# Moving the issue of 28 value-cache tiles from the SyncE queue to GpSimd's queue in a decode-attention kernel

## Chip, core and metric

One core of one Trainium2 chip runs the whole kernel. The metric is the device time of that core in microseconds (us), as a median of runs.

## What is computed

One token (`x`, 448 wide) attends to a key and value cache of 8 heads with 65536 positions of 256 bf16 numbers; each cache head serves two query heads. Beside it runs a small gated feed-forward layer, and a gate `g` mixes the two.

```python
q = (x @ wq)                                # 16 query heads of 256, 8 cache heads
scores = einsum("bhqd,bhkd->bhqk", q, k) * (Dh ** -0.5)
p = softmax(scores)                         # over 65536 positions
o = einsum("bhqk,bhkd->bhqd", p, v)
a = o.reshape(B, Sq, Hq * Dh) @ wo
h = relu(x @ W_gate) * (x @ W_up);  b = h @ W_down
return g * a + (1 - g) * b                  # g = sigmoid(sum(x * gate_w))
```

The two caches are 268 MB each; every byte of them is read once.

## The kernel before

**Tiles and buffers.** Each head's cache is cut into 4 K tiles and 4 V tiles of 128 partitions x 32768 bf16 (8.39 MB, one contiguous 64 KB row per partition), so there are 32 K tiles and 32 V tiles, called K0 to K31 and V0 to V31 here. SBUF holds three such buffers, `ring[0]` to `ring[2]` (L301). `place` (L406) puts K tile n in `ring[1 + n % 2]`, V tiles 0 to 27 in `ring[0]`, and the last four V tiles, for which no K tile is left, in `ring[1]` and `ring[2]`; `wo` comes into `ring[0]` at the end. The weights `wq`, `W_down`, `W_gate` and `W_up` pass through `ring[0]` before V0.

**What is done with a tile.** A K tile is transposed in place by VectorE in four pieces (L529); then TensorE multiplies it with the queries ("QK", L540, 64 matmuls into `ST`), VectorE takes the maximum (L703), and ScalarE the exponential (L705). After the fourth K tile of a head, `P_sb` is rescaled and transposed into `ptp` ("the end of the head", L715 to L760). A V tile needs a slice of `ptp` copied by ScalarE (`pcur`, L591, which also waits for the tile to land) and then 64 matmuls into `O` ("PV", L584).

**What sets the order.** Every operation has a key, a planned time, and each engine's program is sorted by it. On TensorE, K and V work alternate one to one: PV of V0, QK of K4, PV of V1, QK of K5, and so on; V tile i stands beside K tile i + 4. All transfers of tiles are issued by SyncE on one queue, also alternating: K, V, K, V. Before it issues a tile, SyncE waits for TensorE to be done with the tile that had its buffer (`free`, L564): for K tile n the QK of tile n - 2 (L680), for V tile i the PV of tile i - 1 (L772). As SyncE issues in order, a V tile whose buffer isn't free also holds up the K tile behind it.

**Semaphores.** A transfer raises the semaphore of its buffer (`d_r0`, `d_r1`, `d_r2`) by 16. The counts that the other engines wait for are worked out from the plan; TensorE's and ScalarE's inner part is a hardware loop whose wait values are held in registers.

**End.** V28 and V29 wait for the QK of K30 and K31, V30 for the PV of V28; V31 is cut in three pieces (L776) that wait for the PV of V29, and `wo` in six (L785).

The few lines that the prediction follows:

```python
680  kd = dma("sp", t, "r%d" % sl, lambda e: e.dma_start(ring[sl][:], k_src(n)), free(("k", n)))
772  dep = dma("sp", t, "r%d" % sl, lambda e: e.dma_start(ring[sl][:], v_src(n)), free(("v", n)))
567  out_.append(l_[f] if isinstance(f, str) else qk[f[1], 1] if f[0] == "k" else pv[f[1]])
```

Of the kernel before, what the change touches and what calls it, by code (L numbers as in the profile page):

```python
# [27 lines left out]
class _Plan:  # L28
# [14 lines left out]
    def dma(self, eng, key, sem, fn, deps=()):  # L43
        if sem not in self.dsem:
            self.dsem[sem] = self.es.enter_context(self.nc.semaphore("d_" + sem))
        o = _Op(eng, key, fn, deps, dma=sem)
        self.ops.append(o)
        return o
# [212 lines left out]
def bass_gated_mix__gqa_block_cached__glu_gated_reglu__decode_kernel(  # L261
# [22 lines left out]
    NTH = S // TK  # L284
    NT = H * NTH
# [11 lines left out]
    with es:  # L297
# [3 lines left out]
        ring = [sb("ring%d" % i, [128, U * DH], BF) for i in range(NRING)]  # L301
# [69 lines left out]
        op, dma = pl.op, pl.dma  # L371
# [23 lines left out]
        t = 3.0  # L395
# [10 lines left out]
        def place(kind, i):  # L406
            if kind == "k":
                return 1 + i % 2
            if kind == "v":
                return 1 + i % 2 if i >= NT - NTH else 0  # L410
            return {"vp": 2, "wo": 0}[kind]

        for kind, i, _ in order:
            if kind in ("k", "v") or (kind, i) in (("wo", 0), ("vp", 0)):
                r = place(kind, i)
# [105 lines left out]
        def v_src(i):  # L521
            h, a = divmod(i, NTH)
            return A_v_cache[0, h, :, :].rearrange("(t g p u) d -> g p t (u d)", t=NTH, g=NTH, u=U)[a]
# [40 lines left out]
        def free(key):  # L564
            out_ = []
            for f in freed[key]:
                out_.append(l_[f] if isinstance(f, str) else qk[f[1], 1] if f[0] == "k" else pv[f[1]])
            return out_
# [55 lines left out]
        for kind, i, t in sorted(issue, key=lambda q: q[0] != "wq"):  # L624
# [51 lines left out]
            elif kind == "k":  # L676
                n = i
                h, t_ = divmod(n, NTH)
                sl = slot["k", n]
# [88 lines left out]
            elif kind in ("v", "vp"):  # L768
                if kind == "v":
                    n, lo, hi = i, 0, U  # L770
                    sl = slot["v", n]
                    dep = dma("sp", t, "r%d" % sl, lambda e, sl=sl, n=n: e.dma_start(ring[sl][:], v_src(n)), free(("v", n)))  # L772
                else:
                    n, (lo, hi) = NT - 1, PIECES[i]
                    sl = slot["vp", 0]
                    dep = dma("sp", t, ("wq", "wqh", "wd")[i], lambda e, sl=sl, n=n, lo=lo, hi=hi: e.dma_start(  # L776
                        ring[sl][:, lo * 256:hi * 256], v_src(n)[:, :, lo * 256:hi * 256]), free(("vp", 0)))
                args = (n, lo, hi, sl, tL[kind, i], dep)
                if ("tev", n // NTH) in last:
                    make_pv(*args)  # L780
                else:
                    pending.append(args)
            elif kind == "wo":
                lo, hi = WO[i]
                l_["wo", i] = dma("sp", t, "wo%d" % i, lambda e, lo=lo, hi=hi: e.dma_start(  # L785
                    wo_sb[:, lo:hi, :], A_wo.rearrange("(p s) n -> p s n", s=32)[:, lo:hi, :]), free(("wo", 0)))
# [89 lines left out]
```

## Time and profile before

| what | value |
|---|---|
| device time, median of 3 runs | 1275.85 us (1275.74 to 1276.02) |
| profiled execution, first to last instruction (its span) | 1274.3 us |
| difference of the two | 1.55 us |
| bytes moved | 549.13 MB, 431 GB/s over the span |
| DMA queue of SyncE (q1), share of 16 DMA engines' span | 99.7% |
| PE, DVE, ACT, POOL busy | 29%, 49%, 6%, 0% |

The page gives the span of the profiled execution; a device time of that one execution isn't listed apart, so the median stands for it, 1.55 us above. PE is TensorE's matmuls, PEld its weight loads, DVE VectorE, ACT ScalarE, POOL GpSimd, SP SyncE; a name with a q (SPq, ACTq) is the engine's instruction queue, where DMAs are issued. "idle <-X" names what an engine's wait ended on. In rows by window, the last two numbers are the mean busy share of the 16 DMA engines and GB/s; packets are booked in the window in which they start, with their whole time and bytes, so in a very short window the share counts starts and can be far above 1.

### The profile page before, as it was taken

What the parts mean: (1) busy time and instruction counts of PE and PEld (TensorE: products, weight loads), DVE (VectorE), ACT (ScalarE), POOL (GpSimd) and SP (SyncE); (2) the same over time, 40 slices, a digit from 0 to 9 for tenths busy, and PEclk for the clock granted to TensorE, in tenths of its full rate; (3) what the DMA queues carried; (4) which work ended last, traced back from release to release, by engine and by line L of the source; (5) the groups of instructions that cost most, each with busy time, mean ns of one, the idle gap of its engine ahead of it and who ended that gap; (6) DMA issues with size and microseconds to landing.
All of it is one profiled execution on the core that took longest, in us unless ns stands there. A gap on an engine that the chain in (4) does not pass through costs nothing.

```text
span 1274.3 us, 10240 instructions
## 1 busy us (share of the span) xinstructions
PE 365.9 (29%) x4497; PEld 151.4 (12%) x4505; DVE 630.1 (49%) x309; ACT 78.0 (6%) x163; POOL 4.6 (0%) x23
## 2 busy tenths in 40 slices
PE   0534321133320332312233222323302332112525
PEld 0101110011110111101111110111100111001201
DVE  4777655553455633557433565335654355553300
ACT  0001100010000100001000010000000010000100
POOL 1000000000000000000000000000000000000000
PEclk9766665666655666656666656666566666566667
DMA  9999999999999999999999999999999999999998
GB/s 411 430 436 432 426 430 434 432 443 432 430 432 432 434 442 430 430 434 430 438 438 430 430 434 430 440 438 428 430 434 430 444 434 428 430 436 430 442 421 369
DMA packets 11389, 549.13 MB, mean 431 GB/s; under 512 B 1267, under 2 KB 1654, under 8 KB 2294
## 3 DMA queue, kind: packets, MB, share of 16 engines
q1 hardware_dynamic: 11378, 549.03, 99.7%
q8 instruction: 4, 0.07, 0.0%
q14 instruction: 3, 0.02, 0.0%
q10 hardware_dynamic: 4, 0.00, 0.0%
HBM read 549.03 MB, written 0.00 MB: 431 GB/s over the span
## 4 chain that ended last, share of the span: by engine, by line
DMA 81%; PE 16%; DVE 2%; ACT 1%; issue 1%; SPq 0%; ACTq 0%
DMA ring<-in_A_v_cache_dram 74%; PE O L584 13%; DMA ring<-in_A_wo_dram 3%; DMA ring<-in_A_wq_dram 2%; DMA ring<-in_A_k_cache_dram 2%; DVE ring L529 1%; PE ST L540 1%; ACT pcur L591 1%; PE O L501 1%; PE A_ps L551 0%; SPq L785 0%; SPq L776 0%; PE O L653 0%; DVE ring L660 0%; PE A_ps L653 0%
## 5 line engine op out<-in xcount | busy, mean ns | idle before, releaser
L529 DVE STREAM_TRANSPOSE ring<-ring 128x4096 uint32<-128x4096 uint32 x128 | 557.6, 4413 | 196.9 <-DMA ring<-in_A_k_cache_dram 196.9
L584 PE MATMUL O<-ring,pcur 128*4 128x512 bf16 x2048 | 187.3, 545 | 790.4 <-ACT pcur L591 781.9
L703 DVE TENSOR_REDUCE nmb<-ST 128x1 f32<-128x512 f32 x32 | 22.1, 692 | 345.9 <-PE ST L540 345.9
L584 PEld LDWEIGHTS O<-ring,pcur 128*4 128x4 bf16 x2048 | 59.3, 111 | 914.8 <-ACT pcur L591 794.6
L540 PE MATMUL ST<-ring,xcur 128*16 128x512 bf16 x2048 | 136.7, 420 | 44.3 <-DVE ring L529 43.7
L540 PEld LDWEIGHTS ST<-ring,xcur 128*16 128x16 bf16 x2048 | 62.4, 92 | 112.1 <-DVE ring L529 48.6
L705 ACT ACTIVATE P_sb<-ST,nmb 128x512 bf16<-128x512 f32 x32 | 44.6, 1392 | 368.3 <-DVE nmb L703 368.3
L591 ACT COPY pcur<-ptp 128x256 bf16<-128x256 bf16 x32 | 13.2, 415 | 732.6 <-DMA ring<-in_A_v_cache_dram 732.6
L607 DVE TENSOR_SCALAR o_sb<-O,rcm 128x256 bf16<-128x256 f32 x8 | 3.8, 479 | 61.1 <-PE O L584 61.1
L730 DVE TENSOR_TENSOR P_sb<-P_sb,hs 128x1024 bf16<-128x1024 bf16 x16 | 18.9, 1222 | 8.1 <-ACT hs L724 8.1
L735 PE MATMUL PT<-identb,P_sb 128*128 128x128 bf16 x128 | 14.5, 282 | 17.6 <-DVE P_sb L730 17.3
L501 PE MATMUL O<-ring,P_sb 128*128 128x512 bf16 x28 | 8.5, 477 | 17.3 <-DMA ring<-in_A_wq_dram 17.3
L735 PEld LDWEIGHTS PT<-identb,P_sb 128*128 128x128 bf16 x128 | 10.7, 127 | 19.9 <-DVE P_sb L730 19.9
L744 ACT COPY ptp<-PT 128x256 bf16<-128x256 bf16 x32 | 10.3, 375 | 23.0 <-PE PT L735 23.0
L705 ACT ACTIVATION_READ_ACCUMULATOR P_sb<-ST,nmb 128x1 f32 x32 | 8.3, 258 | 0.0
L501 PEld LDWEIGHTS O<-ring,P_sb 128*128 128x128 bf16 x28 | 3.2, 117 | 22.2 <-issue 20.5
L551 PE MATMUL A_ps<-ring,attnA 128*1 128x224 bf16 x64 | 5.3, 322 | 1.1 <-DMA ring<-in_A_wo_dram 1.0
L719 PE MATMUL M_ps<-identf,hs 128*2 128x128 f32 x8 | 2.3, 283 | 10.0 <-DVE hs L717 10.0
L756 DVE RECIPROCAL rc<-M_ps 128x2 f32<-128x2 f32 x8 | 1.4, 171 | 7.5 <-PE M_ps L755 7.5
L755 PE MATMUL M_ps<-hs,ones_f 128*128 128x2 f32 x16 | 4.5, 352 | 0.0
L722 PE MATMUL M_ps<-mx,nselT 2*128 2x1 f32 x16 | 3.2, 268 | 3.0 <-DVE mx L721 3.0
L755 PEld LDWEIGHTS M_ps<-hs,ones_f 128*128 128x128 f32 x16 | 4.0, 311 | 0.0
(93 smaller groups left out, 68.6 us busy)
## 6 DMA issues: line engine op xcount, KB each, us to landing
ring<-in_A_v_cache_dram SPq DMA_DIRECT2D x1, 4096.0 KB, 22.1
ring<-in_A_wq_dram SPq DMA_DIRECT2D x1, 3072.0 KB, 28.9
ring<-in_A_v_cache_dram SPq DMA_DIRECT2D x1, 3072.0 KB, 28.8
ring<-in_B_W_down_dram SPq DMA_DIRECT2D x1, 1568.0 KB, 53.0
ring<-in_B_W_gate_dram SPq DMA_DIRECT2D x1, 1344.0 KB, 26.3
ring<-in_B_W_up_dram SPq DMA_DIRECT2D x1, 1344.0 KB, 29.2
ring<-in_A_wo_dram SPq DMA_DIRECT2D x1, 1232.0 KB, 33.0
ring<-in_A_v_cache_dram SPq DMA_DIRECT2D x1, 1024.0 KB, 30.7
```

Source lines behind the costliest of these rows:

```text
L501: ins = e.matmul(QN_ps, xw3[:, kt, 31 - m:159 - m], rhs, start=(kt == 0 and m == 0), stop=(kt == R3 and m == J // 4 - 1))
L529: return lambda e: e.transpose(v, v)
L540: ins = e.matmul(bank[32 * w:32 * w + 16, :], xcur[:, x0:x0 + 16], ktv[sl][:, u0:u0 + 16, c, :, r_], start=(b == 0 and c == 0 and r_ == 0) ...
L551: ins = e.matmul(A_ps[32 * g:32 * g + 1, 0:D2], lhsT, rhs[:, g * D2:(g + 1) * D2], start=start, stop=stop, skip_group_check=True, tile_pos ...
L584: ins = e.matmul(OP[32 * g:32 * g + 4, :], pcur[a % 2][:, 4 * k:4 * k + 4], ring[sl][:, k * 512:(k + 1) * 512], start=False, stop=False, s ...
L591: pc[n] = op("ap", max(tp - 5, last["tev", h] - 0.5), lambda e: e.copy(pcur[a % 2][:].rearrange("p (k i) -> p k i", i=4), ptp[:].rearrange ...
L703: smax[n] = op("dv", sx, lambda e, n=n, t_=t_: e.tensor_reduce(NM[:, t_:t_ + 1], ST[n % 2][:], AX.X, ALU.max, negate=True), [qk[n, 1], las ...
L705: aexp[n] = op("ac", sx + 1, lambda e, n=n, t_=t_: e.activation(P_sb[:, t_:2048:4], ST[n % 2][:], ACTF.Exp, bias=NM[:, t_:t_ + 1], scale=1 ...
L730: rsc = op("dv", tt, lambda e, pb=pb: e.tensor_tensor(pb, pb, X[:, 12:16].unsqueeze(1).to_broadcast([128, 256, 4]), ALU.mult), [h7, aexp[n]])
L735: ins = e.transpose(PT[rd][:, s * 128:(s + 1) * 128], P_sb[:, (rd * 8 + s) * 128:(rd * 8 + s + 1) * 128], identb[:, :])
L744: ins = e.copy(dst, src)
L755: l3 = mop("pe", T + 19, lambda e: e.matmul(LS_ps, ones_f[:, :], X[:, 6:8], start=True, stop=True), [l2, c_one], tag="l3")
```

## The change

V tiles 0 to 27 are issued by GpSimd (`"gp"`) with semaphores of their own name (`d_v0` in place of `d_r0`, since all 28 lie in `ring[0]`); V28 to V30 stay with SyncE, as do the three pieces of V31. The waits before each issue (`free`) stay what they were. NT - NTH is 28.

```diff
                 if kind == "v":
                     n, lo, hi = i, 0, U
                     sl = slot["v", n]
-                    dep = dma("sp", t, "r%d" % sl, lambda e, sl=sl, n=n: e.dma_start(ring[sl][:], v_src(n)), free(("v", n)))
+                    dep = dma("gp" if n < NT - NTH else "sp", t, ("v%d" if n < NT - NTH else "r%d") % sl, lambda e, sl=sl, n=n: e.dma_start(ring[sl][:], v_src(n)), free(("v", n)))
                 else:
```

SyncE's instructions before, from the last weights on (s_pe counts QK, s_pv counts PV and other work of TensorE; the rows go on alternating K and V):

```order
L640 DMA ring<-in_B_W_up_dram 128x5376
L642 DMA ring<-in_B_W_up_dram 128x896
L680 DMA ring<-in_A_k_cache_dram 128x32768 [waits s_pe] x2
L772 DMA ring<-in_A_v_cache_dram 128x1x32768 [waits s_pv]
L680 DMA ring<-in_A_k_cache_dram 128x32768 [waits s_pe]
```

SyncE's instructions with the change, at the same place and on to the pieces of V31:

```order
L640 DMA ring<-in_B_W_up_dram 128x5376
L642 DMA ring<-in_B_W_up_dram 128x896
L680 DMA ring<-in_A_k_cache_dram 128x32768 [waits s_pe] x29
L772 DMA ring<-in_A_v_cache_dram 128x1x32768 [waits s_pe] x2
L772 DMA ring<-in_A_v_cache_dram 128x1x32768 [waits s_pv]
L776 DMA ring<-in_A_v_cache_dram 128x1x16384 [waits s_pv]
L776 DMA ring<-in_A_v_cache_dram 128x1x12288
L776 DMA ring<-in_A_v_cache_dram 128x1x4096
```

Nothing stands between the K tiles any longer: each waits for the QK that frees its buffer and for no V tile, and V28 follows right behind K31.

GpSimd's instructions with the change, from the last of its set-up on (the buffer's number shown):

```order
L457 TENSOR_TENSOR selc<-selc 128x1 [waits s_gp]
L458 TENSOR_TENSOR selc<-selc 128x1 [waits s_gp]
L459 TENSOR_TENSOR selc<-selc 128x1 [waits s_gp]
L460 TENSOR_SCALAR selc<-selc 128x2 [waits s_gp]
L461 TENSOR_SCALAR selc<-selc 128x2 [waits s_gp]
L772 DMA ring0<-in_A_v_cache_dram 128x1x32768 [waits s_pv] x28
L808 UNCONDITIONAL_BRANCH
```

The 28 V tiles now stand behind GpSimd's set-up, which had been its whole program, each with the wait for the PV before it. TensorE's and VectorE's programs are unchanged; on ScalarE one register instruction falls away, since it waits for another semaphore.

## Prediction

> **What bounds the kernel now.** I read the page's slices first, then its queues, then the share of one long stretch.
>
> ```profile
> DMA  9999999999999999999999999999999999999998
> GB/s 411 430 436 432 426 430 434 432 443 432 430 432 432 434 442 430 430 434 430 438 438 430 430 434 430 440 438 428 430 434 430 444 434 428 430 436 430 442 421 369
> ...
> q1 hardware_dynamic: 11378, 549.03, 99.7%
> ...
> q10 hardware_dynamic: 4, 0.00, 0.0%
> ```
> ```profile
> 300.00:1100.00 800.00, 214.96 (x2805) 91.58 (x2798) 397.88 (x169) 48.85 (x102) 0.00 (x0) 0.62 1.00 434
> ```
>
> The DMA engines have no gap from start to end: share 1.00 at 434 GB/s, while no other engine is busy for half of the stretch. So any microsecond in which they stand still is added to the time, and nothing else is. How they are kept full is seen in the chain of work (start, duration) and in SyncE's own instructions.
>
> ```profile
> 457.27 32.13 DMA ring<-in_A_v_cache_dram
> ...
> 489.43 0.42 ACT pcur L591
> ...
> 495.36 32.74 DMA ring<-in_A_v_cache_dram
> ...
> 528.20 0.42 ACT pcur L591
> ...
> 528.66 6.54 PE O L584 x63
> ...
> 535.21 31.59 DMA ring<-in_A_v_cache_dram
> ```
> ```profile
> 495.36 0.55 SPq L772 DMA_DIRECT2D ring<-in_A_v_cache_dram  x1
> 499.01 0.33 SPq L680 DMA_DIRECT2D ring<-in_A_k_cache_dram  x1
> 535.21 0.55 SPq L772 DMA_DIRECT2D ring<-in_A_v_cache_dram  x1
> 538.93 0.33 SPq L680 DMA_DIRECT2D ring<-in_A_k_cache_dram  x1
> ```
> ```profile
> ring<-in_A_v_cache_dram SPq DMA_DIRECT2D x31, 32.2
> ```
>
> A V tile lands, PV runs, and only then is the next V tile issued. V tiles land 38.7 us apart (from 141.10 for V0 to 1186.11 for V27, below: 1045.0 / 27 = 38.70); the transfer's median is 32.2, so **6.5 us** lie between a landing and the next V issue. The next K issue follows 3.7 us later (499.01 - 495.36, 538.93 - 535.21), since QK stands behind PV on TensorE. In these 6.5 us the DMA engines are fed by the K tile that was issued 3.7 us behind the V tile and passes behind it, whole: two tiles in 38.7 us are 19.35 us each, and the V tile's last byte is followed by 19.35 us of K. That cover is what the strict order buys.
>
> **How two queues share the engines.** One place shows it: ScalarE's queue (q10) loads the two small vectors while K0 passes on SyncE's. Issues, landings and 0.25 us windows of the start:
>
> ```profile
> 0.72 0.42 SPq L680 DMA_DIRECT2D ring<-in_A_k_cache_dram  x1
> ```
> ```profile
> 1.27 0.21 ACTq L422 DMA_DIRECT2D scr<-in_gate_w_dram  x1
> ```
> ```profile
> 10.15 0.61 DVE L464 TENSOR_TENSOR ptp<-P_sb,scr 1x448 f32<-1x448 bf16 x1 [3.93 <-DMA scr<-in_gate_w_dram]
> ...
> 22.81 17.42 DVE L529 STREAM_TRANSPOSE ring<-ring 128x4096 uint32<-128x4096 uint32 x4 [8.20 <-DMA ring<-in_A_k_cache_dram]
> ...
> 102.40 17.42 DVE L529 STREAM_TRANSPOSE ring<-ring 128x4096 uint32<-128x4096 uint32 x4 [1.22 <-DMA ring<-in_A_k_cache_dram]
> ```
> ```profile
> 1.75:2.00 0.25, 0.00 (x0) 0.00 (x0) 0.25 (x1) 0.00 (x0) 0.23 (x1) 1.00 6.44 2097
> ...
> 4.75:5.75 1.00, 0.27 (x5) 0.21 (x5) 0.55 (x4) 0.00 (x0) 0.76 (x4) 1.00 2.42 1049
> 5.75:7.25 1.50, 0.00 (x0) 0.00 (x0) 0.40 (x3) 0.00 (x0) 0.65 (x4) 1.00 0.00 0
> 7.25:7.50 0.25, 0.00 (x0) 0.00 (x0) 0.00 (x0) 0.00 (x0) 0.00 (x0) 1.00 4.24 1839
> ...
> 9.50:10.50 1.00, 0.00 (x0) 0.00 (x0) 0.35 (x1) 0.00 (x0) 0.00 (x0) 1.00 2.42 1049
> ```
>
> 2097 GB/s x 0.25 us are eight packets of 65536 bytes: a packet is one partition's 64 KB row, each of the 16 engines has 8 rows of a tile, and starts come in waves of 16 (1049 GB/s x 1 us), 2.42 us apart (19.35 / 8). `gate_w` was issued at 1.27; its 0.9 KB start only at 7.25 to 7.50 (1839 is seven rows, 1835, and 1 KB), and it counts as landed at 10.15, after a further wave. That reads as strict turns on an engine: `x`, a row of K0, the completion of `x`, a row, `gate_w`, a row, its completion; q10 has four packets. So I take **one 64 KB row per turn, and a turn of its own for the completion**.
>
> [...]
>
> **The change, worked out.** Nothing is removed: same bytes, waits and work. The issue moves from SyncE (0.55 us each) to GpSimd, whose program had 4.6 us of work in all, done by 5 us. K is no longer held behind V. From K0: issued 0.72, first rows 1.75 to 2.00 (1.0 later), landed 22.81, which is 22.1 after the issue, 19.35 for rows and **2.7** around them.
>
> K first runs ahead. While both pass in turns they have equal rates, and in V's 6.5 us K has all of it, so K gains until both K buffers are full and K n + 2 can be issued only behind QK of K n, which stands behind a PV on TensorE. Then a cycle is, from a V landing: 6.5 us to the next V issue; K's issue 3.7 later. V's first row takes 3.1 (starts 1.75, then 4.85, the second wave), so its second is under way when K arrives. Then K, V in turns: K1 V3 K2 V4 ... K6 V8 K7, and V's completion. That is 8 + 7 rows, 15 x 2.42 = 36.3, with 2.7 around them: 6.5 + 2.7 + 36.3 = **45.5 us a cycle instead of 38.7**. One K row is left as cover, and 6.8 us a cycle the DMA engines stand still. K's transposes (17.4 us) begin after the maximum, at 11, and at a head's end about 9 later, so they are done long before the next QK; PV is what K waits for.
>
> Start: V0 is issued behind the weights as before.
>
> ```profile
> 104.18 36.90 DMA ring<-in_A_v_cache_dram
> 141.10 0.04 ACTq L166
> ...
> 147.16 32.62 DMA ring<-in_A_v_cache_dram
> 179.81 0.42 ACT pcur L591
> ...
> 1186.11 0.42 ACT pcur L591
> ...
> 1224.80 0.42 ACT pcur L591
> ```
>
> K3 landed at 102.40, so two rows of K4 are gone by 106.8 when V0 gets its first turn; eight turns each with K4 and K5, 38.7, end at 145.5, and V0 lands at 145.9 (141.1 before). V1 is issued at 152.4 and gets its turn at 155.2, after four rows of K5 alone, with no gap; 16 turns later, at 194.3, it lands (179.8 before: +14.5). From V1 to V27 are 26 cycles of 45.5: V27 lands at 1377.3, before at 1186.1, +191.2. Tail: V29 waits for PV of V27 and QK of K31, 6.5 + 3.7, and takes 22.1 alone: it lands 32.3 behind V27 where 38.7 was (1224.80 - 1186.11), -6.4; the rest stays. Sum against the profiled execution: 1274.3 + 191.2 - 6.4 = 1459.1, and with the 1.55 us between its span and the median of the runs **1460.7**.
>
> **What the trace doesn't show.** GpSimd issues no DMA before, so its delay from wait to first row is open. Lower end: no issue time, -0.55 us a cycle. Upper end: the shares of 16 engines written one after another at its mean instruction (4.6 us / 23 = 0.2), +3.2.
>
> ```profile
> PE 365.9 (29%) x4497; PEld 151.4 (12%) x4505; DVE 630.1 (49%) x309; ACT 78.0 (6%) x163; POOL 4.6 (0%) x23
> ```
>
> I take SyncE's own delay, the nearest row. If V comes more than 0.6 us later (3.7 - 3.1), K's first row stands second, and all eight K rows pass within V's: 47.9 and the delay. If the completion costs no turn, it is 43.1. [...]
>
> **Rivals.**
> First, on the other side: **a whole V tile in one turn.** Then V passes in 19.35, the K tile issued behind it is left whole and covers the 6.5 + 2.7, the engines never stand still: 38.7 a cycle, 1276, no change. It decides from four K rows left at V's landing (9.2 / 2.42 = 3.8). Against it are the waves above; for it, that GpSimd's packets were never seen. [...]
> Second: **K goes faster than V**, if V's rows come in smaller packets. Then V ends alone behind all of K, with no cover: 47.9 a cycle, 26 x 2.4 = 62 more, 1523.
> Third: **two queues move more than one.** Were 434 the limit of one queue, and the best slice (444) what two reach, with the cover kept, 1045 us would shrink by 2.3%, 24 us: 1252. Against it: share 1.00, rows back to back.
>
> **How the numbers follow.** Forecast 0.70 (1398 with a free completion, 1461 - 26 x 2.4; 1549 with a delay of 1.0, 1461 + 26 x 3.4), second rival 0.17, inside that span; first rival 0.09, third 0.04. So the range is 1395 to 1550; 0.13 and some of the delay's upper end stay out. 0.2%, about what a measurement here can tell from no change, is 2.6 us. Faster 0.05 (third rival, and a little of the first), same 0.06, slower 0.89.
>
> **What would show it.** Right: DMA share near 0.85 (38.7 / 45.5), about 370 GB/s in the middle; V landings 45 us apart; K landing 2 to 4 us behind V; SyncE's K issue waiting for QK in each cycle and TensorE never waiting for transposes. Wrong: share 1.00 and 38.7 us cycles (first rival); K landing well before V with V alone at the end (second); above 434 GB/s (third); or another engine late.

## The result, and the profile after

The changed kernel takes 1473.19 us (median of 4 runs, 1467.32 to 1475.78) against 1275.93 before (1275.74 to 1276.10): **1.154 times as long, 95% interval 1.1519 to 1.156**. 1460.7 was predicted. The profiled execution has a span of 1465.2 us and is the fastest of the four (1467.32).

The page after, its slices and queues:

```profile
DMA  9999988898888988879888798888978889888798
GB/s 415 423 449 428 431 349 344 372 430 338 349 354 361 424 349 370 344 345 429 370 344 345 344 429 356 360 344 370 426 324 369 347 367 419 356 356 340 335 412 376
...
q1 hardware_dynamic: 7346, 314.15, 49.7%
q0 software_dynamic: 4032, 234.88, 38.4%
...
q10 hardware_dynamic: 4, 0.00, 0.0%
```

The first five slices are much as before; from V1's cycle on most fall to some 340 to 370 GB/s, and those near 430 are the ones into which hardly any standstill falls. GpSimd's queue appears as q0 with 4032 packets: 28 tiles x 128 rows and 28 x 16 completions, so its packets are 64 KB rows too, like SyncE's. A long stretch in the middle (share and GB/s last; before 1.00 and 434):

```profile
300.00:1300.00 1000.00, 226.83 (x2992) 96.72 (x2993) 423.95 (x184) 51.51 (x110) 11.62 (x22) 0.60 0.87 368
```

One cycle in the chain of work after: V lands, ScalarE's copy, PV, GpSimd's issue, V under way again.

```profile
566.54 39.09 DMA ring<-in_A_v_cache_dram
605.63 0.02 issue
605.65 0.04 ACTq L166
605.69 0.04 issue
605.73 0.42 ACT pcur L591
606.15 0.04 issue
606.20 6.39 PE O L584 x64
612.59 0.28 issue
612.88 39.14 DMA ring<-in_A_v_cache_dram
```

The V transfer's own time is 39.1 us where it was 32.2, and this cycle is 46.3 long (612.88 - 566.54). The mean is 45.7: V1 lands at 194.90 and V27 at 1382.71 (below), 1187.8 / 26. Where the DMA engines stand still is seen in windows of the same cycle:

```profile
604.00:605.00 1.00, 0.00 (x0) 0.00 (x0) 0.00 (x0) 0.00 (x0) 0.00 (x0) 0.50 0.61 262
605.00:606.00 1.00, 0.00 (x0) 0.00 (x0) 0.00 (x0) 0.27 (x1) 0.00 (x0) 0.50 1.82 786
606.00:608.00 2.00, 1.80 (x20) 0.66 (x24) 0.00 (x0) 0.14 (x1) 0.00 (x0) 0.50 0.00 0
608.00:612.00 4.00, 4.00 (x48) 1.29 (x40) 0.00 (x0) 0.00 (x0) 0.00 (x0) 0.53 0.00 0
612.00:614.00 2.00, 2.00 (x42) 0.89 (x37) 0.00 (x0) 0.00 (x0) 0.53 (x1) 1.00 0.00 0
614.00:614.25 0.25, 0.25 (x12) 0.12 (x8) 0.00 (x0) 0.00 (x0) 0.00 (x0) 1.00 8.38 2621
```

Sixteen rows (1.0 MB: 0.26 + 0.79) start between 604 and 606, about when V lands: K's last row on each engine. It is done by about 608, and until 614.0 no row starts, while TensorE runs PV. K's rows cover 2.4 us of the gap and no more.

The trace's DMA records, counted by queue, show the turns themselves. For the tile issued at 566.54, V starts its first row on all 16 engines at 567.8 to 568.8 and its second at 570.9 to 571.6; from 573.3 on each engine starts a row of K after each row of V, 2.42 us apart, until V's eighth. On 9 of the 16 engines K has the third turn, on 7 V has it. On those 7 the 4-byte record of V's completion stands at 602.3 to 603.0, on the 9 at 604.8 to 605.2, each behind a further row of K: the tile lands with its last engines, one row later.

Who waits for whom (DVE's and SyncE's waits):

```profile
DVE ring L529 <- DMA ring<-in_A_k_cache_dram: 26.6, 6, 7.8
```
```profile
SPq L680 <- PE ST L540: 1285.3, 30, 46.5
```

The transposes wait for K 26.6 us in all (196.9 before), and SyncE's K issues wait 1285.3 us in all for QK (191.1 before), 30 of 32, all but the first two. So K is ahead as far as its two buffers allow.

### The profile page after: what moved, and what is told of

The parts are those of the page before. It is cut to its first block, busy times and chain, and to the rows that moved or that the text cites. A ratio compares the mean times of both kernels' runs of the same rounds, so it can differ in the third digit from the quotient of the medians.

```text
span 1465.2 us, 10241 instructions
## 1 busy us (share of the span) xinstructions
PE 363.6 (25%) x4505; PEld 149.0 (10%) x4505; DVE 628.2 (43%) x309; ACT 78.0 (5%) x163; POOL 19.6 (1%) x51
## 3 DMA queue, kind: packets, MB, share of 16 engines
q0 software_dynamic: 4032, 234.88, 38.4%
## 4 chain that ended last, share of the span: by engine, by line
DMA 80%; PE 13%; issue 4%; DVE 1%; ACT 1%; SPq 0%; ACTq 0%; POOL 0%; POOLq 0%
DMA ring<-in_A_v_cache_dram 74%; PE O L584 11%; DMA ring<-in_A_wo_dram 2%; DMA ring<-in_A_wq_dram 2%; DMA ring<-in_A_k_cache_dram 2%; DVE ring L529 1%; PE ST L540 1%; ACT pcur L591 1%; PE O L501 1%; PE A_ps L551 0%; SPq L776 0%; DVE ring L660 0%; PE O L653 0%; PE A_ps L653 0%; ACTq L166 0%
## 5 line engine op out<-in xcount | busy, mean ns | idle before, releaser
L529 DVE STREAM_TRANSPOSE ring<-ring 128x4096 uint32<-128x4096 uint32 x128 | 557.3, 4411 | 28.1 <-DMA ring<-in_A_k_cache_dram 26.6
L584 PE MATMUL O<-ring,pcur 128*4 128x512 bf16 x2048 | 183.4, 536 | 979.8 <-ACT pcur L591 973.4
L772 POOL DMA_DIRECT2D ring<-in_A_v_cache_dram x28 | 15.0, 536 | 1322.2 <-PE O L584 1226.5
L571 PE MATMUL O<-zer,identb 128*128 128x512 bf16 x8 | 4.7, 587 | 0.0
```

The source lines that it names most:

```text
L529: return lambda e: e.transpose(v, v)
L584: ins = e.matmul(OP[32 * g:32 * g + 4, :], pcur[a % 2][:, 4 * k:4 * k + 4], ring[sl][:, k * 512:(k + 1) * 512], start=False, stop=False, s ...
L772: dep = dma("gp" if n < NT - NTH else "sp", t, ("v%d" if n < NT - NTH else "r%d") % sl, lambda e, sl=sl, n=n: e.dma_start(ring[sl][:], v_s ...
```

## The experiments

All times are medians of the kernel's runs. Two theories stand against each other. **Turns**: on each DMA engine the queues take turns packet by packet, so K is spent beside V and nothing covers PV. **GpSimd**: its way of issuing is slow in itself.

**One queue, but GpSimd's.**

```diff
-kd = dma("sp", t, "r%d" % sl, ...)
+kd = dma("gp" if n >= 3 else "sp", t, ("g%d" if n >= 3 else "r%d") % sl, ...)
-dep = dma("sp", t, "r%d" % sl, ...)
+dep = dma("gp", t, ("g%d" if sl else "v%d") % sl, ...)
```

> All tiles from K3 on, K and V alike up to V30, are issued by GpSimd in the old strict order; SyncE keeps the weights, the three pieces of V31 and wo. Theory of turns (the loss comes from K and V taking turns row by row, so that K is nearly spent when V lands): with one queue again, V passes whole and the K tile behind it is the cover. The 0.28 us that GpSimd takes from PV's end to the issue lie under that cover. 1276 us, at most 1285 with the pieces of V31 passing beside V30. Rival (GpSimd's own way of issuing makes transfers slower or later): all 61 tiles now bear that cost, so as slow as the change or slower, 1470 or more.

Measured: 1289.13 us, 1.0102 of before (1.0086 to 1.0119).

```profile
110.00:120.00 10.00, 0.00 (x0) 0.00 (x0) 0.00 (x0) 0.00 (x0) 0.00 (x0) 0.50 0.79 343
120.00:130.00 10.00, 5.87 (x61) 2.69 (x61) 5.20 (x5) 0.00 (x0) 0.00 (x0) 0.50 0.00 1
...
300.00:1100.00 800.00, 220.09 (x2838) 92.66 (x2838) 393.99 (x168) 49.25 (x103) 22.16 (x42) 0.62 1.00 433
```

In the middle the share is 1.00 at 433 GB/s: GpSimd's issue costs nothing there. The 13 us over before, 4 beyond the expectation, come from a place that it had missed: K3 and K4 on the new queue took turns with `W_gate` and `W_up` on SyncE's, these landed late, V0 was issued at 130.5, and some 12 us stood empty. The same turns, at another spot.

**K in half rows, V in half rows, both.** K from K4 on, V tiles 0 to 27:

```diff
-kd = dma("sp", t, "r%d" % sl, lambda e: e.dma_start(ring[sl][:], k_src(n)), ...)
+for q_ in range(2):
+    kd = dma("sp", t + 0.001 * q_, "r%d" % sl, lambda e: e.dma_start(
+        ring[sl][:, q_ * 16384:(q_ + 1) * 16384], k_src(n)[:, q_ * 16384:(q_ + 1) * 16384]), ...)
```

> The change, but each K tile from K4 on is issued as two DMAs of half rows (32 KB per partition), both on SyncE's queue; V tiles keep 64 KB rows on GpSimd's. Theory of turns, one packet per turn: V now moves two bytes for each of K's. In a cycle V's 8 rows are met by only some 7 half rows of K, so about 9 half rows (10.9 us) are left when V lands, more than the 9.5 us without V: no standstill, cycles of about 38.7 us, 1280 to 1300 us. Rival (the queues share by bytes, or GpSimd's issue itself costs the time): no change from 1473, or a little more for 28 more packets of DMA.

> The opposite: each V tile on GpSimd's queue is issued as two DMAs of half rows (32 KB per partition), K tiles keep 64 KB rows. Theory of turns: K moves two bytes for each of V's, all of K passes within V's span and nothing is left as cover; a cycle is 6.8 + 2.7 + 38.7 = 48.2 us instead of the 45.7 measured, 26 x 2.5 = 65 us more than the change: about 1535 us. Rival (sharing by bytes, or a fixed cost per V tile at GpSimd): 1473, or a few us more for the second issue of 0.53 us per tile (28 x 0.53 = 15): up to 1490.

> K tiles from K4 on and V tiles 0 to 27 are both issued as two DMAs of half rows. Theory of turns: turns are equal again, only half as long. V passes 3 half rows before K's first, then 13 of V against 13 of K and the completion's turn: two or three half rows of K are left, 2.4 to 3.6 us, as with one whole row; cycles of 45 to 46 us: 1455 to 1480 us. Rival (issuing K in two parts helps by itself, whatever V's rows are): near the 1296 us of K alone in halves.

Measured: K halves 1295.92 us (ratio 1.0146 to 1.018), V halves 1535.44 (1.2012 to 1.2052), both 1439.45 (1.1269 to 1.1307). The issues (count, KB, us to landing) of K halves, then of V halves:

```profile
ring<-in_A_k_cache_dram SPq DMA_DIRECT2D x56, 4096.0 KB, 36.8
...
ring<-in_A_v_cache_dram POOLq DMA_DIRECT2D x28, 33.0
```
```profile
ring<-in_A_v_cache_dram POOLq DMA_DIRECT2D x56, 4096.0 KB, 37.0
```

The bytes and the two queues are the same in all three; halving K's packets brings V down from 39.1 to 33.0 us and the time back to within 2% of before, halving V's adds 62 us to the change (65 expected). In these runs the rate goes by packets, not by bytes. With both halved the time is 16 us below the low end expected: in most cycles of that run V lands 37.7 us behind its first issue, 1.5 us earlier than in the change (39.2), and 26 x 1.5 = 39 covers the 34 us between 1473 and 1439. The step that the expectation had wrong is the start: by the DMA records of two cycles V passes four or five half rows before K's first, by engine, and not three. Of the 20 us that K halves keeps above before, some 10 are in the tail, where V29 waits for PV and QK and no row starts from 1210 to 1220 us.

**K held back by its own transposes.**

```diff
-kd = dma("sp", ..., free(("k", n)))
+kd = dma("sp", ..., free(("k", n)) + ([last["tr"]] if n > NTH else []))
 tr = [op("dv", tk + 4.5 * w, f_trans(sl, w), [kd]) for w in range(4)]
+last["tr"] = tr[1]
```

> The change, but SyncE holds each K tile from K5 on until VectorE has done two of the four transposes of the K tile before it, some 9 us later than now (18 at a head's end). Nothing else differs. Theory of turns: V passes some 5 rows alone, so about 4 or 5 K rows are left when V lands (9.7 to 12 us), enough to cover the 9.5 us without V: cycles near 38.7 us, except at heads' ends, where K comes late and some 3 us stand still 7 times: 1280 to 1310 us. Rival (GpSimd's issue itself costs the time, or simply that K waits too long): a later K can only add: 1473 or more, up to 1473 + 27 x 9 = 1716.

> The late K of the run before, but the hold begins with K8, when K has run ahead. Theory of turns, with the 47 us that the slices of 130 to 300 us lost there put down to the hold itself (from K5 on it kept a single K tile under way, which landed beside V): the start is now as in the change (V landings about 145, 195 and 240 us), then no standstill except at heads' ends and at the tail: 1300 to 1320 us. Rival (the excess of the late K over 1276 is spread over all cycles): 1344 as before, or the change's extra at the start on top, up to 1360.

 (here the condition is `n >= 2 * NTH`)

Measured: 1343.72 us and 1368.37 us. Both expectations missed, the second in its reason too. The late K, by stretches:

```profile
100.00:300.00 200.00, 56.67 (x603) 19.82 (x603) 93.11 (x36) 9.40 (x20) 2.88 (x5) 0.59 0.84 356
...
500.00:900.00 400.00, 129.81 (x1340) 42.02 (x1340) 196.88 (x78) 21.79 (x46) 5.30 (x10) 0.62 0.99 423
```

From 500 us on it does what was said: share 0.99 where the change has 0.87. At its start it doesn't. GpSimd's V issues there, SyncE's K issue beside the second of them, and the stretch before it:

```profile
148.00 0.54 POOL L773 DMA_DIRECT2D ring<-in_A_v_cache_dram  x1 [45.18 <-PE O L584]
195.63 0.53 POOL L773 DMA_DIRECT2D ring<-in_A_v_cache_dram  x1 [47.09 <-PE O L584]
```
```profile
194.77 0.33 SPq L680 DMA_DIRECT2D ring<-in_A_k_cache_dram  x1
```
```profile
187.00:195.00 8.00, 6.18 (x64) 2.07 (x68) 8.00 (x3) 0.42 (x1) 0.00 (x0) 0.52 0.00 0
```

K is issued 0.9 us before V: the two start together, pass in turns, land together, and both gaps fall together (no row starts from 187 to 195), in a cycle of 47.6 us (195.63 - 148.00). Since a held K follows its own landing by some 9 us and V its own by some 7, K drifts behind V from cycle to cycle; by V7 it is 10 us behind, and its rows cover the gap. The five runs of the second hold lie from 1364.5 to 1452.7, and the trace is of the longest: there K drifts until it meets the next V at 564 us and stays with it for a dozen cycles of 47.7 us. How far that holds for the shorter runs isn't shown. So the hold was a wait of its own, and these two runs say little on the question.

**The queues swapped.**

```diff
-kd = dma("sp", t, "r%d" % sl, ...)
+kd = dma("gp" if n >= 4 else "sp", t, ("g%d" if n >= 4 else "r%d") % sl, ...)
```

(V tiles stay with SyncE, as before the change.)

> The two queues swapped: K tiles from K4 on are issued by GpSimd, all V tiles by SyncE. Theory of turns: which queue carries which makes no difference, since each gets one row per turn; only V's issue no longer bears GpSimd's 0.28 us behind PV (SyncE: 0.02), 27 x 0.26 = 7 us less than the change: about 1466 us. Rival (GpSimd's queue is served worse than SyncE's, in rate or delay): now K is the slow one, more of it is left when V lands, and the time falls well below, under 1420 us.

Measured: 1405.21 us (ratio 1.0989 to 1.1026): 68 below the change, on the rival's side. Two issues of V, which SyncE makes, in the chain:

```profile
552.91 37.02 DMA ring<-in_A_v_cache_dram
...
596.41 37.02 DMA ring<-in_A_v_cache_dram
```

V takes 37.0 us, not 39.1: 2.1 us, about one row (2.4). The swap has moved K's issue from 3.4 us behind V's (616.27 - 612.88 in the change) to 4.0 us. Either GpSimd's queue is served worse, or 4.0 us is late enough for V to pass one row more alone. The next three tell these apart with V on GpSimd as in the change.

**K 0.7 us later, 2.2 us later, 8 us later.** K waits for the maximum (`smax[n - 2]`), for the exponential (`aexp[n - 2]`), or for 18 small copies on GpSimd behind V's issue:

```diff
-kd = dma("sp", ..., free(("k", n)))
+kd = dma("sp", ..., free(("k", n)) + ([smax[n - 2]] if n >= NTH else []))
```
```diff
+if 0 < n < NT - NTH:
+    g_ = last.get(("gd", n - 1), l_["xm"])
+    for i_ in range(18):
+        g_ = op("gp", t + 0.001 * (i_ + 1), lambda e: e.tensor_scalar(scr[:, 0:128], identf[:], 1.0, None, ALU.mult), [g_])
+    last["gd", n] = g_
...
+kd = dma("sp", ..., free(("k", n)) + [last.get(("gd", n - 5))])
```

> The change, but each K tile from K4 on is issued behind VectorE's maximum of the tile two before it (L703, 0.69 us) and no longer right behind its QK: K's issue comes some 4.15 us behind V's where the change has 3.45. In the runs so far V takes about 39.2 us when K is issued less than 3.9 us behind it and 36.9 when it is more: one K row more is left when V lands. Theory of turns: a delay of 0.7 us in each K issue makes each of 26 cycles one row shorter, 2.2 to 2.4 us: 1473 - 57 to 62, about 1412 to 1416 us. Rival (the 39 and 37 us have another cause, such as the queue that carries K): 1473, or 0.7 x 27 = 19 more.

> As the run before, but K waits for ScalarE's exponential (L705), so that it comes some 5.6 to 5.9 us behind V's issue. Theory of turns in whole rows: the next border is one row on, at 3.9 + 2.4 = 6.3, so nothing changes against 4.15: V takes 36.9 us and the time is that of the run before, about 1415 us. Rival (the gain is in proportion to the delay): 1473 - 26 x 2.3 = 1413 too, or, at 1 us for each us of delay, some 40 us less than with 4.15.

> The change, but K is held back by a fixed time behind V's issue and not by K's own transposes: GpSimd runs 18 small copies in a row behind each V issue (0.53 us each in the start of the profile, 9.5 us or somewhat more) and SyncE issues the K tile when they are done, some 10 to 12 us behind V. Theory of turns: three borders (3.9, 6.3, 8.7) or four (11.2) are passed, V takes 32 us or 30, four or five K rows (9.7 to 12.1 us) are left when it lands and cover the 9.5 us without V; the offset is tied to V and can't drift as the hold on the transposes did: cycles near 38.7 us, 1280 to 1300 us. Rival (a held-back K costs time, as 1344 to 1368 us of the two holds on the transposes may be read): above 1340 us.

Measured: 1423.26 us (ratio 1.1138 to 1.1175), 1421.18 (1.113 to 1.117), 1312.86 (1.0277 to 1.0313). With the maximum, V's and K's issue and V's transfer:

```profile
595.28 0.53 POOL L772 DMA_DIRECT2D ring<-in_A_v_cache_dram  x1 [43.36 <-PE O L584]
```
```profile
599.48 0.33 SPq L680 DMA_DIRECT2D ring<-in_A_k_cache_dram  x1
```
```profile
595.28 36.77 DMA ring<-in_A_v_cache_dram
```

V is on GpSimd's queue, as in the change, and takes 36.8 us since K comes 4.2 us behind it: the offset does it, not the queue. A wait of 0.7 us more in each K issue makes the kernel 50 us faster, and another 1.5 us changes it by 2 us (5.65 us behind V, 36.9 us): steps of whole rows. Both times lie some 6 or 7 us above what was expected; with the maximum PV and its wait take 6.8 us between a landing and the next issue, 6.4 in the change, and 26 x 0.4 = 10. With some 11.6 us of offset the stretch from 300 to 1100 us has:

```profile
300.00:1100.00 800.00, 211.87 (x2714) 88.66 (x2718) 395.37 (x167) 47.92 (x101) 208.86 (x380) 0.61 0.99 427
```

Share 0.99, with two queues and V on GpSimd. Of the 37 us left above before, 13 more than the 1300 expected at most, some 13 are the tail again and some 13 are 427 GB/s in place of 434 over 800 us; the rest stays open. None of the runs on two queues is faster than the one queue of before.

**Half of PV left out.**

```diff
-for k in range(lo // 2, hi // 2):
+for k in range(lo // 2, hi // 2 if n >= NT - NTH else hi // 4):
```

> The change with half of PV left out for V0 to V27: only the first 32 of 64 matmuls per tile run (the output lacks the other positions). Theory: PV, which before lay under K's transfer, now lies bare in each cycle between V's landing and the next V issue, so each us taken from it is a us of time: half of some 5.6 us, 2.8 x 27 = 76 less than the change: about 1397 us. Rival (the DMA engines stand still for another reason, so that PV is still covered): 1473, unchanged.

Measured: 1373.97 us (ratio 1.0737 to 1.0778), 99 below the change where 76 was expected. PV has come to lie bare. It fell to 3.6 us, some 2.1 less than the change's mean of about 5.7 (57 us over 27 cycles). Most of the rest is V's transfer again, since K's issue now comes 3.7 to 4.4 us behind V's: 16 of the tiles from V2 on take about 37 us, 34 us in all, and the others 39.2.

```profile
454.91 36.88 DMA ring<-in_A_v_cache_dram
491.89 0.42 ACT pcur L591
492.36 3.61 PE O L584 x25
496.25 39.47 DMA ring<-in_A_v_cache_dram
```

## Why the prediction was right

**Direction, mechanism and size held.** The start and the end of the chain after:

```profile
102.43 43.06 DMA ring<-in_A_v_cache_dram
145.49 0.02 issue
...
152.43 42.47 DMA ring<-in_A_v_cache_dram
194.90 0.02 issue
...
1382.71 0.02 issue
...
1392.28 22.75 DMA ring<-in_A_v_cache_dram
1415.03 0.02 issue
```

- *The start*: V0 landed at 145.5 (145.9 predicted), V1 at 194.9 (194.3).
- *The cycle*: 45.7 (45.5). V's transfer, 2.7 + 36.3 = 39.0 in the sum, is 39.1.
- *The tail*: V29 landed 32.3 us behind V27 (32.3).
- *The sum*: V27 landed at 1382.7, not 1377.3. 26 x 0.2 is nearly all of the difference, and this all but 1 us of what the span misses (1465.2 against 1459.1). It lies in the transfer, 39.2 us in the mean where 39.0 was put: V's first rows start 1.2 us after the issue, K0's 1.0. The gap from a landing to the next issue is 6.4 (6.5 in the sum): GpSimd adds 0.28 us between PV's end and its issue, where SyncE has 0.02, but PV itself takes 5.7 us instead of 5.9. Of the other 8 us to 1473.19, 2.1 lie between span and time of the profiled execution (1467.32), and 5.9 are its being the fastest of four; why the changed kernel's runs spread over 8.5 us and those before over 0.4 isn't known.
- *The start of the trace*, from which the turns were inferred, was read wrongly in one place: by the records the completion of `x` comes at 1.67, before K0's first row, and not between two rows. `gate_w` then waited for two rows of K0, and its completion for one, as was said. GpSimd's set-up ends at 6.6 and not by 5 us, long before V0's issue at 102.4, so nothing hangs on it.
- *The delay of GpSimd's queue*: no run shows the 1.0 us with which the forecast reached 1549, nor the 3.2 of the upper end. V's first rows start 1.2 us after GpSimd's issue, where K0's start 1.0 after SyncE's, and the issue itself comes 0.28 us behind PV.
- *The unit of a turn*: halving K's packets (1295.92 us), V's (1535.44) and both (1439.45) moved the time as turns of one packet say. In the change's trace a turn is one row of 64 KB: rows of K and V alternate 2.42 us apart.
- *The first rival*, a tile in one turn, falls with V's 39.1 us. Two queues moved nearly what one did (427 GB/s with K 8 us later, 434 before), but the change's time did not stay, since V's 32.2 us became 39.1.
- *The second*, K faster than V, falls with q0's rows of 64 KB, as large as K's; V halves shows what it would have cost: 1535 (1523 predicted). *The third* falls with the stretch from 300 to 1100 us: 434 GB/s before, 427 where two queues keep the share at 0.99 (K 8 us later), 431 with K halves.

**One step was set too roughly, and that it did no harm is luck.** The sum gives K's first row the third turn. By its own figures that turn comes 1.0 + 3.1 + 2.4 = 6.5 us after V's issue, and K, issued 3.7 behind V, would be ready at 4.7, 1.8 us before. In the runs the turn is settled earlier: by the DMA records of V2 to V26 in the change, the swap, half of PV and the two waits for maximum and exponential, K has it on at least one engine of each tile when issued up to 3.8 us behind V, and on none from 4.1 on, where V takes 37 us. The change's offset is 3.4 and not 3.7, because GpSimd's 0.28 us stand before V's issue, so it lies half a microsecond from cycles that are 2 us shorter; at 3.7 it would have been 0.1 to 0.4. The swap's miss comes from that.

## What to carry to other kernels

In this kernel, whose DMA engines never rested before (share 1.00), the order in which transfers queued covered the 6.5 us between a tile's landing and the next issue to its buffer with 19.35 us of K. On two queues that passed side by side both landed at nearly the same time (V at 605.6, K's last rows by about 608), the cover was down to 2.4 us, and 1275.93 us became 1473.19. Before a stream is split off, ask how many rows of the other are left when its tile lands, and compare them with the gap. Where the streams were on two queues, what helped here was an offset between their issues that was tied to the one with the single buffer (some 11.6 us: 1312.86 us), or smaller packets on the one that should yield (half rows of K: 1295.92 us).

## What the runs showed of the hardware

- An engine's next row reads as settled about when it starts the one before. In the change V's first rows start 1.2 us after V's issue, the second 4.1 to 5.4, the third turn comes 2.4 later. K, issued 3.4 behind V, would be ready at about 4.4, with K0's 1.0 us from issue to first row. By the DMA records of V2 to V26 it has the third turn on 4 to 10 of the 16 engines, and V on the others, though that turn starts only at 6.5 or later. With K 4.2 us behind V (ready at 5.2), V has it on all 16 for each of these tiles. The start of the kernel agrees: `gate_w`, issued at 1.27, lets K0's second row pass, which starts at 4.88. That the choice is made a row ahead is read from these counts; no record shows the moment itself.
- One engine of 16 was enough to make a tile land later: in the swap K has the third turn on one engine only beside V3 and V9, and these take 39.6 us where the other tiles from V2 to V26 take 36.9 to 37.3. In the change the tile issued at 566.54 has the last record of V's completion at 605.2 and lands at 605.6.
- So the time moved in steps of one row (V's transfer 39.1, then 36.8 and 36.9 us): 0.7 us more of waiting in each cycle took 50 us off (1473.19 to 1423.26), 1.5 us more only 2 (1421.18).
- In the holds on the transposes two queues whose waits followed their own landings fell into step, at an offset at which both gaps fell together: 47.6 us for a cycle at the start of the first (148.00 to 195.63), and a dozen cycles of 47.7 in the longest run of the second.
